# Layer 1 of the last two token groups: three units of four column tiles by seven products of halves

## The chip, the cores and the metric

The kernel runs on one core of a Trainium2 chip. The metric is the device time of one execution in microseconds (us); less is better.

## The reference

Attention with a relative-position bias for 8 batches, 8 heads, 576 positions and 64 numbers per head, followed by a feed-forward block on the 4608 rows of 512 numbers that it gives:

```python
scores = q @ k.T / 8 + bias_table[bucket(|i - j|)]
x = softmax(scores) @ v            # (8, 8, 576, 64) -> (4608, 512)
h = np.maximum(x @ w_in, 0.0)      # layer 1: 512 -> 2048
out = (h * h) @ w_out              # layer 2: 2048 -> 512
```

The change is in layer 1, `relu(x @ w_in)` and the squaring, for the last 1024 of the 4608 rows.

## The kernel before

The kernel writes down every operation with its engine, an estimated duration, what it depends on, the buffers it takes and a due time (`P.add`). A planner (`Plan.schedule`) then gives each engine a fixed order: the operation that can begin first goes first, and among those the one with the earliest due time. The engines execute that order; the planner's times themselves play no part on the chip, and semaphores hold an instruction back until its data is there. Each engine works its own queue strictly in order.

Attention goes by 32 pairs of heads (`pair(p)`, four to a batch): scores on TensorE (PE) into the PSUM tiles `sets_ps` (two tiles `st0`, `st1` of two banks each), exponentials on ScalarE (ACT) into one of three large buffers `pt`, the bias as a factor on VectorE (DVE), then `pv` matmuls and the division by the sum. The result `xs` is turned by a transposing DMA into `xt_sb` (512 numbers on 4 x 128 partitions, tokens along the row).

The two layers go by nine groups of 512 tokens (`layers(g)`, g from 0 to 8). Layer 1 of a group is 16 column tiles `nt` of 128 outputs. Each is a "quartet" of four matmuls (`f1`, line 1102: four slices `kk` of the 512 inputs, 512 tokens), into one of three banks `f` (`g_ps`). ACT takes the ReLU out of PSUM into `rt` (line 1123), and DVE squares it into `g` (line 1133), the group's activations.

Layer 2 (`second(g)`, line 1017) already goes by seven products of half matrices in place of eight (Winograd's form of Strassen's scheme): with the sums of activations `s` made on DVE (`sums_of_activations`, line 972) and sums of weights `wt` made once, products 1, 2, 6, 5, 7, 3, 4 go into PSUM, in two blocks of eight matmuls over 256 columns each, and DVE (line 1045) or ACT (line 1051) reads them into `y`, adding what was read before. Layer 2 of group g - 1 is planned among layer 1 of group g. In the last group it stands alone at the end.

The last `pv` matmuls end at 311.5 us of the profiled execution. After that only layer 2 of group 6 (its end), layer 1 of groups 7 and 8, and layer 2 of groups 7 and 8 are left. The three `pt` buffers and the two `st` tiles have no further use then.

Of the kernel before, what the change touches and what calls it, by code (L numbers as in the profile page):

```python
# [10 lines left out]
FP32 = mybir.dt.float32  # L11
FP16 = mybir.dt.float16
EXPF = mybir.ActivationFunctionType.Exp
RELUF = mybir.ActivationFunctionType.Relu
COPYF = mybir.ActivationFunctionType.Copy
MULT = mybir.AluOpType.mult

B, H, S, D = 8, 8, 576, 64
# [7 lines left out]
GT = 512  # L26
NG = B * S // GT
XB = 3
XR = XB * S
# [10 lines left out]
SIX = 2  # L40
V_EARLY, V_HW = 18900.0, 2
LATE2 = 7000
T_POOL, T_DUE = 0, 0
ORDER = "k0 i0 q1 q0 v i1 o0 k1 i2 o1 o2 i3 o3"
HALF = GT // 2
# [135 lines left out]
def mm(n):  # L181
    return n / 2.4 + 2.5


def act(n):
    return 174.0 + n / 1.2


def dve(n, rate=1.0, fix=160.0):
    return fix + n / (0.96 * rate)  # L190
# [3 lines left out]
def kernel(  # L194
# [10 lines left out]
    nc = tc.nc  # L205
    assert (_bucket(np.arange(128, S)) == NBK - 1).all()

    def io(ins):
        tc.keep_in_program_order(ins)
        return ins  # L210
# [16 lines left out]
    w_in_sb = sb("w_in_sb", [128, 4, 2048])  # L227
# [13 lines left out]
    pt_sb, pm_sb = sb("pt", [128, NPT, PW + 64]), sb("pm", [128, NPT, S + 64])  # L241
# [4 lines left out]
    xt_sb = sb("xt", [128, 4, XR + 64])  # L246
    wt_sb = sb("wt", [128, 3, 8, 256])
    ss = {i: sb(f"s{i}", [128, 8, 2, 128]) for i in (1, 2, 4)}
    gs = [sb(f"g{i}", [128, 16, GT]) for i in range(NGB)]
# [4 lines left out]
    rts = [sb(f"rt{i}", [128, GT]) for i in range(NRT)]  # L254
# [29 lines left out]
    def one_of(engs, fn, deps, bufs, due):  # L284
        op = P.add(engs, None, deps, bufs, due)
        op.fn = lambda: fn(op)
        return op
# [322 lines left out]

    xt_ready, x_last = {}, {}
    x_bufs = {}

    def copy_to(engs_n, out_f, in_f, deps, bufs, due, fp16=True, dve_only=False):

# [13 lines left out]
    def pair(p):  # L629
# [190 lines left out]
        for part, qt0, nq in ((0, 0, 3), (1, 3, 2)):  # L820
            bank = Buf(r_pv)

            def pv(qt0=qt0, nq=nq, bank=bank):
                ps = pv_ps[bank.slot][:, 0 : nq * 130].rearrange("p (t e d) -> p t e d", t=nq, e=2)
                pt, pm = pts[pb.slot], p4s[pb.slot]
                va, vm = vas[b_v[b].slot], v4s[b_v[b].slot]
                for i in range(nq):
                    c = (qt0 + i) * 128
                    io(
                        nc.tensor.matmul(  # L830
                            ps[:, i, :, :], pm[:, c : c + 128], vm[:, hp, :, 0:65], start=True, stop=False
                        )
                    )
                    for e in range(2):
                        for jt in range(4):
                            io(
                                nc.tensor.matmul(  # L837
                                    ps[:, i, e, :],
                                    pt[:, (2 * jt + e) * S + c : (2 * jt + e) * S + c + 128],
                                    va[:, jt, 2 * hp + e, 0:65],  # L840
                                    start=False,
                                    stop=(jt == 3 and e == 1),
                                )
                            )

            o = P.add(
                {"PE": nq * 300.0}, pv,
                bands + list(exps.values()) + l_v[b, hp] + first, [bank, pb, b_v[b]], T + 1, after, "f",
            )
            rb = Buf(r_r)  # L850

            def recip(nq=nq, bank=bank, rb=rb):
                ps = pv_ps[bank.slot][:, 0 : nq * 130].rearrange("p (t e d) -> p t e d", t=nq, e=2)
                io(nc.vector.reciprocal(out=rs[rb.slot][:, 0:nq], in_=ps[:, :, :, 64:65]))

            def norm(nq=nq, bank=bank, rb=rb, qt0=qt0):
                ps = pv_ps[bank.slot][:, 0 : nq * 130].rearrange("p (t e d) -> p t e d", t=nq, e=2)
                io(
                    nc.vector.tensor_tensor(  # L859
                        out=xs[xb.slot][:, qt0 : qt0 + nq, :].rearrange("p t (e d) -> p t e d", e=2),  # L860
                        in0=ps[:, :, :, 0:64],
                        in1=rs[rb.slot][:, 0:nq].to_broadcast([128, nq, 2, 64]),
                        op=MULT,
                    )
                )

            o = P.add({"DVE": 200.0}, recip, [o], [bank, rb], T - 2000)
            o = P.add({"DVE": dve(nq * 128)}, norm, [o], [bank, rb, xb], T - 2000)
            norms.append(o)
            if b >= DT_X:  # L870
                c = (b % XB) * S + 128 * qt0
                t = P.add(
                    {"SP": 1320.0},
                    lambda qt0=qt0, nq=nq, c=c: io(
                        nc.sync.dma_start_transpose(
                            out=xt_sb[:, hp, c : c + 128 * nq].rearrange("p (t d) -> p t d", d=128), in_=xs[xb.slot][:, qt0 : qt0 + nq, :].rearrange("p t d -> p (t d)")
                        )
                    ),
                    [o, x_last.get((hp, 1 - part))] + xt_free(b * S + 128 * (qt0 + nq)), [xb], T - 2000,
                )  # L880
                t = x_last[hp, part] = P.add({"DMA": 232.0 * nq}, None, [t], [xb], -1e9)
                end = b * S + min(128 * (qt0 + nq), S) - 1
                for g_ in range((b * S + 128 * qt0) // GT, end // GT + 1):
                    xt_ready.setdefault(g_, []).append(t)
# [48 lines left out]
    def sums_of_weights():  # L933
# [21 lines left out]
            done.append(o)  # L955
        return done

    def sums_of_activations(g):

        gb = g_bufs[g]  # L960
        sb_ = s_bufs[g] = {i: Buf(r_s[i]) for i in (1, 2, 4)}
        for c0 in (0, 4):
            o = None
            for to, uses in ((1, [1]), (2, [1, 2]), (4, [2, 4]), (3, [])):

                def add(to=to, c0=c0):
                    a11, a12, a21, a22 = (fourth(gb, eo, t, c0, 4) for t in range(2) for eo in range(2))
                    s = {i: ss[i][:, c0 : c0 + 4] for i in (1, 2, 4)}
                    out_, a, b_ = {
                        1: (s[1], a21, a22), 2: (s[2], a11, s[1]), 4: (s[4], a12, s[2]), 3: (a21, a21, a11)  # L970
                    }[to]
                    io(nc.vector.tensor_tensor(out=out_, in0=a, in1=b_, op=mybir.AluOpType.subtract))  # L972

                o = P.add(
                    {"DVE": dve(1024, 2.0)}, add, squares[g][2 * c0 : 2 * c0 + 8] + [o],
                    [gb] + [sb_[i] for i in uses], G0 + GP * g - 5e4,
                )
                s_done.setdefault((g, to), []).append(o)

    def second(g):  # L980
# [25 lines left out]
        for i in (int(x) for x in (P_LAST if g == NG - 1 else P_ORDER).split()):  # L1006
# [4 lines left out]
            for s_ in range(2):  # L1011
# [10 lines left out]
                        )  # L1022

                def atom(d, i=i, s_=s_, bf=bf, ns=ns, mul=mul, own=own):
                    deps = d + [x for n in ns for x in s_done[g, n]] + squares[g]
                    deps += read_of[before[i]] if i in before and not own else []
                    deps += l_wout if i in (1, 2) else t_done
                    return P.add(
                        {"PE": 8 * mm(HALF)}, mul, deps, [bf, gb] + [sb_[n] for n in ns if n != 3], 1e6, 0.0, "f",
                    )  # L1030
# [50 lines left out]
                atoms.append(fin)  # L1081
        return atoms

    def layers(g):

        due = G0 + GP * g
# [2 lines left out]
        if g < NG:  # L1089
            g_bufs[g] = Buf(r_gb)  # L1090
            gb1 = g_bufs[g]
            squares[g] = []
            for nt in range(16):
                bank = Buf(r_g)

                def f1(nt=nt, bank=bank):
                    c = (g * GT) % XR
                    n = min(GT, XR - c)
                    for a, z, c in ((0, n, c), (n, GT, 0)):
                        for kk in range(4 if z > a else 0):  # L1100
                            io(
                                nc.tensor.matmul(  # L1102
                                    g_ps[bank.slot][:, a:z], w_in_sb[:, kk, ts(nt, 128)],
                                    xt_sb[:, kk, c : c + z - a],
                                    start=(kk == 0), stop=(kk == 3),
                                )
                            )

                atoms1.append((nt, f1, bank))
        i2 = 0  # L1110
        last = None
        for i in range(16):
            if i < len(atoms1):
                nt, f1, bank = atoms1[i]
                o = P.add(
                    {"PE": 4 * mm(512)}, f1, xt_ready[g] + [l_win[nt // 4]], [bank, gb1], due + i * 2000, 0.0, "f"
                )
# [3 lines left out]
                def relu(o, bank=bank, rb=rb):  # L1121
# [4 lines left out]

                engs = {"ACT": act(512), "DVE": dve(512)} if g < RELU_DVE else {"ACT": act(512)}
                r = one_of(engs, relu, [o], [bank, rb], 0.0)
                squares[g].append(
                    P.add(  # L1130
                        {"DVE": dve(512, 2.0)},
                        lambda rb=rb, nt=nt, gb1=gb1: io(
# [64 lines left out]
```

## Time and profile before

| what | value |
|---|---|
| three runs | 372.94, 373.65, 372.58 us; median 372.94 |
| profiled execution | 372.94 us, of them a span of 371.1 us from the first to the last instruction |
| PE busy | 355.1 us (96%), 3930 matmuls |
| DVE busy | 265.8 us (72%) |
| ACT busy | 257.5 us (69%) |
| granted PE clock | 0.999 |
| last matmul | issued by about 368.0 us |

A row of the timeline gives start, duration, engine, line, operation, output and inputs with their shapes, and in brackets how long the engine was idle before it and which instruction ended that idle time. Matmuls are pipelined: the row of a merged run of matmuls also holds the time in which the last one drains, so the distance between starts is what a matmul costs PE. In the chain of work that ended last that part is left out. "Issue" as a releaser means that nothing in the profile held the engine back.

### The profile page before, as it was taken

The page shows a single profiled execution, that of the slowest core. Times are in us where ns is not written, and L with a number is a line of the kernel's source. Part 1 is how long each engine was busy: PE and PEld are TensorE (multiplying, and loading weights), DVE is VectorE, ACT ScalarE, POOL GpSimd, SP SyncE. Part 2 cuts the span into 40 slices and gives each one's busy share as a digit, 9 for nine tenths or more (in the row PEclk, how much of TensorE's full clock was granted, in tenths as well). Part 3 has the DMA queues.
Part 4 walks back from the last instruction along what each step waited for, and adds up shares of the span by engine and source line. Part 5 has one row for each costly group of instructions (what it writes and reads, how often), then busy time and mean ns, then how long its engine had stood idle before and what let it go on. Part 6 is the DMA issues. An engine that isn't in the chain of part 4 may idle for free.

```text
span 371.1 us, 9910 instructions
## 1 busy us (share of the span) xinstructions
PE 355.1 (96%) x3930; PEld 242.0 (65%) x3930; DVE 265.8 (72%) x594; ACT 257.5 (69%) x367; POOL 186.5 (50%) x343
## 2 busy tenths in 40 slices
PE   3978999899999999999999999999999999999996
PEld 2655555556587457877785468745877688546785
DVE  3997789957785598668965797569765985583573
ACT  4998989688575887679766887688659870564220
POOL 7897359194665686757846557667624100000000
PEclk9999999999999999999999999999999999999999
DMA  8999999595999999998999999999965224100022
GB/s 164 153 133 170 195 178 94 82 123 93 181 134 126 148 149 128 133 159 163 121 135 147 104 160 135 133 163 153 122 105 125 53 50 72 57 2 28 30 85 87
DMA packets 162292, 44.25 MB, mean 119 GB/s; under 512 B 145734, under 2 KB 162246, under 8 KB 162246
## 3 DMA queue, kind: packets, MB, share of 16 engines
q0 software_dynamic: 74208, 14.53, 50.7%
q1 hardware_dynamic: 87696, 28.80, 41.3%
q8 instruction: 31, 0.51, 0.6%
q10 hardware_dynamic: 342, 0.30, 0.3%
q14 instruction: 15, 0.12, 0.1%
HBM read 36.88 MB, written 9.44 MB: 125 GB/s over the span
## 4 chain that ended last, share of the span: by engine, by line
PE 86%; DVE 4%; DMA 4%; ACT 2%; POOL 2%; issue 1%; POOLq 0%; ACTq 0%
PE f L1102 34%; PE f L1017 29%; PE pv L837 9%; PE st L702 8%; PE pv L830 2%; DMA w_in_sb<-in_moe_w_in_dram 2%; PE st L751 2%; PE st L726 1%; DMA ks<-in_k_dram 1%; DVE pt L794 1%; ACT pt L713 1%; DVE x L859 1%; POOL ks L276 1%; DVE s L972 1%; POOL qs L276 1%
## 5 line engine op out<-in xcount | busy, mean ns | idle before, releaser
L713 ACT ACTIVATE pt<-st 128x1024 f16<-128x1024 f32 x128 | 127.4, 1025 | 30.4 <-PE st L702 30.4
L1102 PE MATMUL f<-xt,w_in_sb 128*128 128x512 f16 (+4 forms) x704 | 138.6, 341 | 0.2 <-ACT xt L619 0.2
L1123 ACT ACTIVATE rt<-f 128x512 f16<-128x512 f32 x144 | 85.2, 602 | 49.3 <-PE f L1102 44.0
L1102 PEld LDWEIGHTS <-w_in_sb 128*128 128x128 f16 x704 | 62.6, 98 | 57.3 <-issue 12.2
L1133 DVE TENSOR_TENSOR g<-rt 128x512 f16<-128x512 f16 x144 | 64.9, 455 | 36.6 <-ACT rt L1123 35.9
L794 DVE TENSOR_TENSOR pt<-pt,tb_sb 128x1536 f16<-128x1536 f16 (+2 forms) x96 | 60.1, 635 | 14.8 <-ACT pt L713 14.1
L1017 PEld LDWEIGHTS <-g 128*128 128x128 f16 x576 | 54.6, 98 | 14.4 <-issue 4.7
L276 POOL DMA_DIRECT2D qs<-in_q_dram x79 | 55.4, 714 | 4.0 <-DMA w_out_sb<-in_moe_w_out_dram 2.5
L276 POOL DMA_DIRECT2D ks<-in_k_dram x79 | 55.2, 702 | 1.4 <-issue 1.2
L837 PE MATMUL pv<-va,pt 128*128 128x65 f16 x1280 | 54.6, 193 | 0.0
L837 PEld LDWEIGHTS <-pt 128*128 128x128 f16 x1280 | 50.2, 97 | 2.7 <-issue 1.0
L1045 DVE SCALAR_TENSOR_TENSOR y<-f,y 128x512 f32<-128x512 f32 (+1 forms) x47 | 31.4, 667 | 22.9 <-PE f L1017 21.5
L1017 PEld LDWEIGHTS <-s 128*128 128x128 f16 x432 | 41.2, 98 | 9.8 <-issue 2.5
L702 PE MATMUL st<-qt,kt 64*128 64x512 f16 x256 | 40.5, 387 | 0.8 <-ACT pm L761 0.4
L684 POOL COPY qz<-qt 64x64 f16<-64x64 f16 x61 | 19.1, 313 | 39.8 <-DMA qt<-qs 31.4
L684 POOL COPY qz<-kt 64x64 f16<-64x64 f16 x58 | 18.7, 322 | 38.9 <-DMA kt<-ks 30.4
L1017 PE MATMUL f<-wt,g 128*128 128x256 f16 x288 | 36.2, 273 | 0.0
L1017 PE MATMUL f<-w_out_sb,s 128*128 128x256 f16 x288 | 36.1, 273 | 0.0
L830 PE MATMUL pv<-vm,pm 128*128 128x130 f16 x160 | 35.3, 221 | 0.7 <-DVE x L859 0.6
L1017 PE MATMUL f<-w_out_sb,g 128*128 128x256 f16 x272 | 34.5, 273 | 0.7 <-ACT y L1051 0.7
L859 DVE TENSOR_TENSOR x<-pv,r 128x384 f16<-128x384 f32 x64 | 31.4, 490 | 2.0
L972 DVE TENSOR_TENSOR s<-g,s 128x1024 f16<-128x1024 f16 x36 | 26.0, 723 | 0.4
(66 smaller groups left out, 284.9 us busy)
## 6 DMA issues: line engine op xcount, KB each, us to landing
out_dram<-y SPq DMA_DIRECT2D x34, 256.0 KB, 2.3
f<-in_v_dram SPq DMA_DIRECT2D x24, 256.0 KB, 4.4
qs<-in_q_dram POOLq DMA_DIRECT2D x48, 64.0 KB, 4.5
ks<-in_k_dram POOLq DMA_DIRECT2D x48, 64.0 KB, 3.6
w_in_sb<-in_moe_w_in_dram POOLq DMA_DIRECT2D x4, 512.0 KB, 7.6
w_out_sb<-in_moe_w_out_dram POOLq DMA_DIRECT2D x4, 512.0 KB, 10.2
qs<-in_q_dram POOLq DMA_DIRECT2D x7, 144.0 KB, 5.0
ks<-in_k_dram POOLq DMA_DIRECT2D x7, 144.0 KB, 6.2
```

The source lines that it names most:

```text
L276: lambda: io(eng.dma_start(out=out_(), in_=in_())),
L684: io(eng.tensor_copy(out=dst[qb.slot][rw, rw], in_=src[qb.slot][rw, 512:576]))
L702: nc.tensor.matmul(sets_ps[st.slot][:, e, :], kt[rw, ts(jt, 128)], qt[rw, 0:512], start=True, stop=True,)
L713: nc.scalar.activation(out=p5(pts[pb.slot])[:, jt, :, 0:512], in_=sets_ps[st.slot], func=EXPF, scale=SCALE)
L794: io(nc.vector.tensor_tensor(out=a, in0=a, in1=t, op=MULT))
L830: nc.tensor.matmul(ps[:, i, :, :], pm[:, c : c + 128], vm[:, hp, :, 0:65], start=True, stop=False)
L837: nc.tensor.matmul(ps[:, i, e, :], pt[:, (2 * jt + e) * S + c : (2 * jt + e) * S + c + 128], va[:, jt, 2 * hp + e, 0:65], start=False, sto ...
L859: nc.vector.tensor_tensor(out=xs[xb.slot][:, qt0 : qt0 + nq, :].rearrange("p t (e d) -> p t e d", e=2), in0=ps[:, :, :, 0:64], in1=rs[rb.s ...
L1017: nc.tensor.matmul(home[bf.slot][:, ts(s_, HALF)], left(c, s_), right(c), start=(c == 0 and (s_ == 0 or apart) and (own or i not in before ...
L1102: nc.tensor.matmul(g_ps[bank.slot][:, a:z], w_in_sb[:, kk, ts(nt, 128)], xt_sb[:, kk, c : c + z - a], start=(kk == 0), stop=(kk == 3),)
L1123: io(nc.scalar.activation(out=rts[rb.slot], in_=g_ps[bank.slot], func=RELUF))
L1133: nc.vector.tensor_tensor(out=gs[gb1.slot][:, nt, :], in0=rts[rb.slot], in1=rts[rb.slot], op=MULT)
```

## The change

A "unit" here is two neighbouring column tiles of the first 1024 columns of `w_in` and the two that lie 1024 columns further on, for all 512 tokens of a group: in the kernel before, 4 quartets (16 matmuls of 512 columns). The changed kernel computes two units of group 7 (tiles 0 to 3 and 8 to 11) and one unit of group 8 (tiles 0, 1, 8, 9) by seven products of halves: the 512 inputs are halved (k), the columns (i) and the tokens (j) as well. A product is four matmuls over 256 columns. The other 8 tiles of group 7 and 12 of group 8 stay quartets.

The sums that this needs (four of tokens `t` for each group, four of weights `s` for each pair of tiles, the latter shared by the two groups) are made by DVE into the room of the `pt` buffers, once the last `pv` matmuls are done. The products go into the four banks of `st0` and `st1`: products 1 (with 2 added on top) and 6 into the two banks of one tile, 5 (then 3) and 7 (then 4) into those of the other. They are read by ACT (product 1 by a copy, product 2 by a ReLU) or by DVE, which adds a partial sum `y` read before; those `y` too lie in the room of `pt`. Sums that are results then get a ReLU on ACT, in place in `rt`, and a square on DVE or ACT, whichever the planner finds free. The dependence on the squares is now kept by tile. Nothing is changed in attention, layer 2's arithmetic or any DMA.

```diff
+UNITS = {7: 2, 8: 1}
+USTEP = 700.0
...
+    pv_last = []
...
+            if p >= 4 * B - 3:
+                pv_last.append(o)
...
+    def made(g, a, z):
+        return [x for nt in range(a, z) for x in squares[g][nt]]
...
-                    {"DVE": dve(1024, 2.0)}, add, squares[g][2 * c0 : 2 * c0 + 8] + [o],
+                    {"DVE": dve(1024, 2.0)}, add, made(g, 2 * c0, 2 * c0 + 8) + [o],
...
-                    deps = d + [x for n in ns for x in s_done[g, n]] + squares[g]
+                    deps = d + [x for n in ns for x in s_done[g, n]] + made(g, 0, 16)
...
+    late, r_late = {}, Ring(4)
+    def late_room():
+        a, b_, c_ = (pt_sb[:, i, 0:4096] for i in range(3))
+        assert max(UNITS.values()) <= 2
+        for i in range(1, 5):
+            late["s", i] = a[:, ts(i - 1, 1024)].rearrange("p (k c) -> p k c", k=2)
+            late["y", i - 1] = b_.bitcast(FP32)[:, ts(i - 1, 512)]
+        for g in UNITS:
+            for i in range(1, 5):
+                o = ((g - min(UNITS)) * 4 + i - 1) * 512
+                late["t", g, i] = c_[:, o : o + 512].rearrange("p (k c) -> p k c", k=2)
+    def late_sums(n, dst, terms, deps, due):
+        o, made_ = None, []
+        for i, (a, b_, op) in terms:
+            o = P.add(
+                {"DVE": dve(n, 2.0)},
+                lambda i=i, a=a, b_=b_, op=op: io(nc.vector.tensor_tensor(out=dst(i), in0=a(), in1=b_(), op=op)),
+                deps + [o], (), due,
+            )
+            made_.append(o)
+        return made_
+    SUB = mybir.AluOpType.subtract
+    def by_sevens(g, units, due):
+        if not late:
+            late_room()
+        c = (g * GT) % XR
+        assert c + GT <= XR
+        wq = lambda i, k, u: w_in_sb[:, 2 * k : 2 * k + 2, 1024 * i + 256 * u : 1024 * i + 256 * u + 256]
+        xq = lambda k, j: xt_sb[:, 2 * k : 2 * k + 2, c + HALF * j : c + HALF * j + HALF]
+        t = lambda i: late["t", g, i]
+        t_ops = late_sums(
+            512, t,
+            [
+                (1, (lambda: xq(0, 1), lambda: xq(0, 0), SUB)),
+                (2, (lambda: xq(1, 1), lambda: t(1), SUB)),
+                (4, (lambda: xq(1, 0), lambda: t(2), SUB)),
+                (3, (lambda: xq(1, 1), lambda: xq(0, 1), SUB)),
+            ],
+            xt_ready[g] + pv_last, due - 1e5,
+        )
+        gb1 = g_bufs[g]
+        for u in range(units):
+            s_ = lambda i, u=u: late["s", i][:, :, ts(u, 256)]
+            if ("ops", u) not in late:
+                late["ops", u] = late_sums(
+                    512, s_,
+                    [
+                        (1, (lambda u=u: wq(1, 0, u), lambda u=u: wq(1, 1, u), mybir.AluOpType.add)),
+                        (2, (lambda s_=s_: s_(1), lambda u=u: wq(0, 0, u), SUB)),
+                        (4, (lambda u=u: wq(0, 1, u), lambda s_=s_: s_(2), SUB)),
+                        (3, (lambda u=u: wq(0, 0, u), lambda u=u: wq(1, 0, u), SUB)),
+                    ],
+                    l_win + pv_last, due - 1e5 + 10.0 * u,
+                )
+            sets = {"ab": Buf(r_set), "cd": Buf(r_set)}
+            y = {i: Buf(r_late) for i in "uv"}
+            prod = {
+                1: ("a", lambda u=u: wq(0, 0, u), lambda: xq(0, 0), True),
+                6: ("b", lambda s_=s_: s_(2), lambda: t(2), True),
+                2: ("a", lambda u=u: wq(0, 1, u), lambda: xq(1, 0), False),
+                5: ("c", lambda s_=s_: s_(1), lambda: t(1), True),
+                7: ("d", lambda s_=s_: s_(3), lambda: t(3), True),
+                3: ("c", lambda s_=s_: s_(4), lambda: xq(1, 1), False),
+                4: ("d", lambda u=u: wq(1, 1, u), lambda: t(4), False),
+            }
+            reads = {
+                1: ("u", None, None), 6: ("u", "u", None), 2: (None, None, (0, 0)), 5: ("v", "u", None),
+                7: (None, "v", (1, 1)), 3: (None, "u", (0, 1)), 4: (None, "u", (1, 0)),
+            }
+            after_read = {2: 1, 3: 5, 4: 7}
+            read_of = {}
+            for n, i in enumerate((1, 6, 2, 5, 7, 3, 4)):
+                bk, left, right, first_ = prod[i]
+                st = sets["ab" if bk in "ab" else "cd"]
+                ps = lambda st=st, bk=bk: sets_ps[st.slot][:, "abcd".index(bk) % 2, :]
+                def mul(left=left, right=right, first_=first_, ps=ps):
+                    for f in range(2):
+                        for kk in range(2):
+                            io(
+                                nc.tensor.matmul(
+                                    ps()[:, ts(f, HALF)], left()[:, kk, ts(f, 128)], right()[:, kk, :],
+                                    start=(first_ and f == 0 and kk == 0), stop=(kk == 1), skip_group_check=True,
+                                )
+                            )
+                o = f1_last[g] = P.add(
+                    {"PE": 4 * mm(HALF)}, mul,
+                    xt_ready[g] + t_ops + late["ops", u] + (read_of[after_read[i]] if i in after_read else []),
+                    [st, gb1], due + (7 * u + n) * USTEP, 0.0, "f",
+                )
+                to, plus, where = reads[i]
+                deps = [o]
+                if plus == "u":
+                    deps += read_of[1 if i == 6 else 6]
+                if plus == "v":
+                    deps += read_of[5]
+                bufs = [st] + [y[x] for x in {to, plus} - {None}]
+                rb = Buf(r_rt) if where else None
+                bufs += [rb] if rb else []
+                def ev(e, to=to, plus=plus, ps=ps, y=y, rb=rb):
+                    dst = rts[rb.slot] if rb else late["y", y[to].slot]
+                    if plus is not None:
+                        io(
+                            nc.vector.scalar_tensor_tensor(
+                                out=dst, in0=ps(), scalar=1.0, in1=late["y", y[plus].slot], op0=MULT, op1=mybir.AluOpType.add
+                            )
+                        )
+                    else:
+                        io(nc.scalar.activation(out=dst, in_=ps(), func=RELUF if rb else COPYF))
+                e = one_of({"DVE": dve(512)} if plus else {"ACT": act(512)}, ev, deps, bufs, 0.0)
+                read_of[i] = [e]
+                if not rb:
+                    continue
+                if plus is not None:
+                    e = P.add(
+                        {"ACT": act(512)},
+                        lambda rb=rb: io(nc.scalar.activation(out=rts[rb.slot], in_=rts[rb.slot], func=RELUF)),
+                        [e], [rb], 0.0,
+                    )
+                def square(o, rb=rb, where=where, u=u):
+                    src = rts[rb.slot].rearrange("p (f s) -> p f s", f=2)
+                    n0 = 8 * where[0] + 2 * u
+                    dst = gs[gb1.slot][:, n0 : n0 + 2, ts(where[1], HALF)]
+                    if o.eng == "ACT":
+                        io(nc.scalar.activation(out=dst, in_=src, func=SQUAREF))
+                    else:
+                        io(nc.vector.tensor_tensor(out=dst, in0=src, in1=src, op=MULT))
+                e = one_of({"DVE": dve(512, 2.0), "ACT": act(512)}, square, [e], [rb, gb1], due - 1e5)
+                for f in range(2):
+                    squares[g][8 * where[0] + 2 * u + f].append(e)
     def layers(g):
...
-            squares[g] = []
-            for nt in range(16):
+            squares[g] = {nt: [] for nt in range(16)}
+            units = UNITS.get(g, 0)
+            for nt in [nt for nt in range(16) if nt % 8 >= 2 * units]:
...
                 atoms1.append((nt, f1, bank))
+            if units:
+                by_sevens(g, units, due)
...
+        skip = 16 - len(atoms1) if g < NG else 0
         for i in range(16):
-            if i < len(atoms1):
-                nt, f1, bank = atoms1[i]
+            if i >= skip and g < NG:
+                nt, f1, bank = atoms1[i - skip]
...
-                squares[g].append(
+                squares[g][nt].append(
```

More of the change, by code (lines that the diff above doesn't have):

```diff
@@ L14 @@
 RELUF = mybir.ActivationFunctionType.Relu
+SQUAREF = mybir.ActivationFunctionType.Square
 COPYF = mybir.ActivationFunctionType.Copy
```

## The prediction

> **What bounds the kernel now.** I read the page's forty slices first, then the chain of work that ended last, then the windows of the last 58 us, then single rows of the timeline there. The built order of both programs is the same on SyncE and GpSimd throughout, and on TensorE, VectorE and ScalarE up to about 312 us, so only the tail can move.
>
> ```profile
> PE   3978999899999999999999999999999999999996
> DVE  3997789957785598668965797569765985583573
> ACT  4998989688575887679766887688659870564220
> ```
>
> ```profile
> 313.00:318.00 5.00, 5.00 (x37) 3.33 (x35) 1.66 (x4) 1.55 (x3) 0.00 (x0) 1.00 0.42 124
> 318.00:333.00 15.00, 15.00 (x74) 6.93 (x72) 10.70 (x24) 9.79 (x17) 0.00 (x0) 1.00 0.05 17
> 333.00:357.00 24.00, 24.00 (x175) 16.93 (x174) 12.96 (x26) 8.96 (x15) 0.00 (x0) 1.00 0.10 34
> ```
>
> The columns are the stretch, its length, then busy time of PE, weight loads, DVE, ACT, POOL, then the granted clock, the DMA share and GB/s. From 313 us PE is busy for the whole of each stretch at full clock, while DVE and ACT have room. The chain says the same: one unbroken run of matmuls.
>
> ```profile
> 318.48 14.68 PE f L1102 x68
> 333.15 0.87 PE f L1017 x8
> 359.24 8.75 PE f L1017 x80
> ```
>
> So here a matmul column taken out is time won, and a wait put in front of PE is time lost. In the before there is no such wait.
>
> **What it takes away.** A unit was 4 column tiles of layer 1, each a quartet of matmuls over 512 tokens. A quartet takes 0.866 us start to start (14.68 us over 17 quartets is 0.864), so 3.46 us a unit. It becomes 7 products of 4 matmuls over 256 columns. That shape stands in layer 2: 80 matmuls in 8.75 us, 0.109 us each, so a product is 0.436 us and a unit 28 x 0.109 = 3.05 us. Saved: 0.41 us a unit, 1.23 us for three units. The operands (w_in, xt, and sums in pt) are new in this shape; half of a 512 matmul (0.108) and the 0.109 row bound it closely. The built order has 36 more matmuls, which is 3 x (28 - 16): the change does what it says.
>
> A rule speaks against the exchange: the Trainium skill, "TensorE: Matmul & The Clock Gate", section "Back-to-back issue gap", puts sustained pairs of weight load and matmul at about 131 ns for 512 columns and 81 ns for 128, so small moving operands pay for their weight loads. By it, as an estimate with 98 ns put in for 256, a unit would cost 0.6 us more instead of less. The rows above show 216 and 109 ns, in proportion, and they decide.
>
> **What it adds beside PE.** DVE: 16 sums in half precision (4 for each group's tokens, 4 for each of the two weight slices) at 0.41 us each (a 512-element sum of two SBUF operands has such rows), 15 additions out of PSUM at 0.69 us, less 6 squares of 0.42 us that go to ACT: 14 us. ACT: 3 copies and 6 squares more at 0.60 us: 5 us. The squares and the ReLU from SBUF have no row; 0.60 us (PSUM source) is the nearest, and taking 0.42 to 0.70 moves the result by less than 0.1 us, as most lie beside matmuls. The 4 sums for group 7 and the first weight slice fit DVE's gaps between 312 and 317 us (it is busy 1.66 us of 313 to 318), ahead of the first product that reads them at 317.9. GpSimd and SyncE get nothing, and no DMA is moved. So the volume is covered; what counts is waits.
>
> **The waits.** These rows price one hop each: four matmuls, then ACT reading their bank, then DVE reading what ACT wrote.
>
> ```profile
> 313.98 1.03 PE L1102 MATMUL f<-xt,w_in_sb 128*128 128x512 f16 x4
> 315.04 0.60 ACT L1123 ACTIVATE rt<-f 128x512 f16<-128x512 f32 x1 [9.34 <-PE f L1102]
> 315.67 0.42 DVE L1133 TENSOR_TENSOR g<-rt 128x512 f16<-128x512 f16 x1 [0.80 <-ACT rt L1123]
> 140.61 0.42 DVE L859 TENSOR_TENSOR x<-pv,r 128x256 f16<-128x256 f32 x1
> 141.09 0.22 PE L830 MATMUL pv<-vm,pm 128*128 128x130 f16 x1 [0.21 <-DVE x L859]
> L1045 DVE SCALAR_TENSOR_TENSOR y<-f,y 128x512 f32<-128x512 f32 x11 | 7.6, 689 | 5.4 <-PE f L1017 4.3 <-DMA xt<-x 1.1
> ```
>
> From the end of issue of the last matmul (313.98 + 0.87 = 314.85) to ACT's start is 0.20; ACT to DVE 0.03; DVE to PE 0.06.
>
> By the built order the products of the first and third unit run 1, 6, 5, 7, 2, then other work, 3, 4; of the second 1, 6, other work, 2, 5, 7, a quartet, 3, a quartet, 4. Products 1 and 6 lie in the two banks of one PSUM tile, 5 and 7 in those of the other. In the built program, waits go by tile and not by bank: ACT's copy of product 1 waits for product 6 too, and product 2 (which accumulates onto 1) waits for the addition that reads product 6. So product 2 can start only after product 6, copy, addition:
> 0.20 + 0.60 + 0.03 + 0.69 + 0.05 = 1.57 us after 6 has been issued.
> PE has products 5 and 7 meanwhile: 0.87 us. Stall 0.70 us. Queued behind product 2 on PE stands everything else, the plain quartets too, as the queue is in order. In the same way product 3 waits for the additions that read 5 and then 7 (0.20 + 0.69 + 0.03 + 0.69 + 0.05 = 1.66 us after 7), and product 4 for the one that reads 3 (0.94 us after 3).
>
> I walked the three queues of the built order from 312 us with these durations. The same walk of the before gives no stall and an end of PE at 368.04 us; the trace has 359.24 + 8.75 = 367.99. For the changed order it gives:
> - group 7, first unit: product 2 stalls 0.69; products 3 and 4 have two plain quartets (1.73) ahead of them and stall nothing;
> - group 7, second unit: between 6 and 2 stand a quartet and a block of layer 2 (1.74), but ACT and DVE are still finishing the first unit: 0.22; product 3 has only one quartet (0.87) against 1.66: 0.79; product 4, a quartet against 0.94: 0.07;
> - group 8, its unit: product 2 again 0.69; product 3 0.13; product 4 0.06.
>
> Sum 2.65 us. Net: 2.65 - 1.23 = +1.42 us. After the last product (about 341 us) the walk has no more waits: all of layer 1 is now ahead of layer 2's products 6 to 4 of group 7, which run 8.7 us and cover the squares and sums of group 8. The 1.42 us therefore reaches the end, and the output DMAs follow as before. The profiled execution took 372.94 us (span 371.1 and 1.84 around it), which is also the median of the three runs. So 372.94 + 1.42 = 374.4 us.
>
> Bounds: if nothing queued on ACT and DVE and each hop cost nothing, only the three large stalls would be left, about 0.6 + 0.65 + 0.6, and the net would be +0.6 us (373.6). If each of the seven waits cost 0.1 us and each of its additions 0.05 us more, the stalls would be 3.7 us, the net +2.5 (375.4).
>
> **The rivals.** A difference of under 0.3% (1.12 us) is about what a measurement of this kernel can't tell from no change.
>
> *No wait decides* (other side, faster). If product 2 waited for the copy of product 1 alone, the chain would be 0.20 + 0.60 + 0.05 = 0.85 us counted from product 1, and products 6, 5 and 7 (1.31) would cover it; with the like for 3 and 4 only the 1.23 us would be left: 371.7 us. It decides when the stalls of a unit are below 0.41 us. For it: DVE's free 4.3 of 15 us and ACT's 5.2. Against it: the waits of the built order are by tile, and idle time elsewhere does not shorten a chain of dependent steps. Chance 0.07.
>
> *Stalls and saving nearly cancel.* Stalls between 0.1 and 2.35 us, for instance if the 0.79 or one of the 0.69 is absent because a plain quartet that follows has cover: about 373.6 us. Chance 0.26.
>
> *More than the walk.* Square might need another function table than the one loaded at the start, which took 1.28 us here: 375.7 us with one more load. The built order has no further load. The Trainium skill, "ScalarE: Activation LUTs", section "Table sets: the hidden batching unit", gives about 2.7 us for a switch; the one load in this trace took 1.28 us, and that is what I use. Or ACT, with 9.79 us busy of 15 before, falls behind on group 7 and holds layer 2's first product: that product stands at about 334.2, the last square of group 7 at about 332.7, so ACT and DVE may be 1.5 us late before this costs. Chance 0.05, 375 to 376 us.
>
> *The forecast*, 1.1 to 2.5 us slower: chance 0.62.
>
> **How the numbers follow.** Slower by over 0.3%: forecast and the last rival, 0.67. Within 0.3%: 0.26. Faster: 0.07. The range: bounds 373.6 to 375.4, widened at the low end into the cancelling case, and by the scatter of the medians (runs from 372.58 to 373.65): 373.1 to 375.5. Outside it I leave the faster rival, the low end of the cancelling case and the far tail of the last, under 0.2.
>
> **What would show it.** Right: PE idle 2.2 to 3.2 us in all before the new matmuls, released by DVE; three waits of 0.6 to 0.9 us (two before product 2 at about 319.9 and 338.2, one before product 3 at about 328.7); new products 0.109 us a matmul; the run from the last layer-2 matmul to the end unchanged; clock still 1.00. Wrong: no idle PE between 318 and 342 us (then faster), new matmuls above 0.115 us (saving gone without any wait), a second table load, or a wait in front of group 7's layer 2.

## The result, and the profile after

The changed kernel takes 375.07 us (median of 6 runs, 374.18 to 375.31), the kernel before 372.81 us beside it (6 runs): ratio 1.0054, 95% interval 1.0040 to 1.0069, so 1.5 to 2.6 us slower. Forecast was 374.4 us, slower, in a range of 373.1 to 375.5.

The slices and two of the stretches of the changed kernel, in the same columns as before:

```profile
PE   3978999899999999999999999999999999999996
DVE  3897789967775598668865786579755877788773
ACT  4998989688575887679767887688568860777300
318.00:333.00 15.00, 13.73 (x94) 9.00 (x93) 11.72 (x24) 11.19 (x21) 0.00 (x0) 1.00 0.06 19
333.00:357.00 24.00, 23.41 (x174) 16.79 (x173) 20.15 (x41) 11.78 (x21) 0.00 (x0) 1.00 0.06 21
```

The slices still show 9 for PE up to the last one: a tenth of a slice is 0.9 us, and the new waits are shorter. Only the stretches show that PE now pauses: 13.73 of 15 us and 23.41 of 24, where both had been full. The clock stays at 1.00. DVE's work has grown from 12.96 to 20.15 of the 24 us of the second stretch and still leaves it idle time.

PE's own timeline from the first new product to the last (start, duration, line, output and inputs, runs merged; line 1183 is a new product, 1258 a plain quartet, 1027 layer 2):

```profile
318.03 0.60 PE L1183 MATMUL st<-xt,w_in_sb 128*128 128x256 f16 x4
318.46 1.47 PE L1183 MATMUL st<-pt 128*128 128x256 f16 x12
320.52 0.60 PE L1183 MATMUL st<-xt,w_in_sb 128*128 128x256 f16 x4 [0.59 <-DVE pt L1208]
...
325.30 1.04 PE L1027 MATMUL f<-wt,g 128*128 128x256 f16 x8
326.38 0.60 PE L1183 MATMUL st<-xt,w_in_sb 128*128 128x256 f16 x4
326.81 1.04 PE L1183 MATMUL st<-pt 128*128 128x256 f16 x8
327.69 1.03 PE L1258 MATMUL f<-xt,w_in_sb 128*128 128x512 f16 x4
329.35 0.60 PE L1183 MATMUL st<-xt,pt 128*128 128x256 f16 x4 [0.64 <-DVE rt L1208]
329.79 1.03 PE L1258 MATMUL f<-xt,w_in_sb 128*128 128x512 f16 x4
330.80 0.60 PE L1183 MATMUL st<-pt,w_in_sb 128*128 128x256 f16 x4
...
336.87 1.47 PE L1183 MATMUL st<-pt 128*128 128x256 f16 x12
338.88 0.60 PE L1183 MATMUL st<-xt,w_in_sb 128*128 128x256 f16 x4 [0.54 <-DVE pt L1208]
```

Products 6, 5 and 7 start at 318.46 and need 12 x 0.109 = 1.31 us; product 2 could begin at 319.77 and begins at 320.52. That is a wait of 0.75 us. The bracket says 0.59, because the profile lets a matmul's row last 0.16 us longer than its place in the queue. Read in this way, from start to start, the waits before the new products are 0.75, 0.21, 0.80, 0.15, 0.70, 0.21 and 0.07 us, 2.9 in all. The brackets alone would give 1.8.

The start of that first wait, as it looks on the two engines that end it:

```profile
319.15 0.60 ACT L1213 ACTIVATE pt<-st 128x512 f32<-128x512 f32 x1 [0.33 <-PE st L1183]
319.78 1.49 DVE L1208 SCALAR_TENSOR_TENSOR pt<-st,pt 128x512 f32<-128x512 f32 x2 [0.50 <-ACT pt L1213]
```

Product 1 was issued by 318.46, but ACT's copy of it begins at 319.15, after product 6 (issued by 318.90, drained 0.16 us later); DVE's first addition begins 0.03 us after the copy, and PE goes on 0.05 us after that addition (319.78 + 0.69 = 320.47).

From the first matmul of group 7's layer 1 to the start of the last block of layer 2 the kernel before took 366.06 - 313.98 = 52.08 us, the changed one 368.34 - 314.56 = 53.78: +1.70 us. On PE the built order differs in this stretch and nowhere else. The remaining 0.6 us of the two profiled spans lies ahead of it, where both kernels do the same; the experiments show how much that part varies by itself.

### The profile page after: what moved, and what is told of

It reads as the page before. It is cut to its first block, busy times and chain, and to the rows that moved or that the text cites. A ratio compares the mean times of both kernels' runs of the same rounds, so it can differ in the third digit from the quotient of the medians.

```text
span 373.4 us, 10016 instructions
## 1 busy us (share of the span) xinstructions
PE 355.4 (95%) x3966; PEld 245.9 (66%) x3966; DVE 278.0 (74%) x619; ACT 261.6 (70%) x376; POOL 185.3 (50%) x343
## 4 chain that ended last, share of the span: by engine, by line
PE 85%; DVE 9%; DMA 3%; ACT 2%; issue 1%; ACTq 0%; DVEq 0%
PE f L1258 31%; PE f L1027 27%; PE pv L841 9%; PE st L706 8%; PE pv L834 2%; PE st L1183 2%; DVE pt L798 2%; PE st L755 2%; DMA xt<-x 1%; PE st L730 1%; DVE x L865 1%; DMA g<-in_q_dram 1%; DVE pt L1208 1%; PE f L661 1%; DVE rt L1208 1%; ACT pm L765 1%
## 5 line engine op out<-in xcount | busy, mean ns | idle before, releaser
L717 ACT ACTIVATE pt<-st 128x1024 f16<-128x1024 f32 x128 | 127.4, 1024 | 30.9 <-PE st L706 30.8
L1258 PE MATMUL f<-xt,w_in_sb 128*128 128x512 f16 (+4 forms) x656 | 127.5, 338 | 0.7 <-DMA xt<-x 0.4
L1282 ACT ACTIVATE rt<-f 128x512 f16<-128x512 f32 x132 | 77.8, 601 | 34.7 <-PE f L1258 30.8
L1258 PEld LDWEIGHTS <-w_in_sb 128*128 128x128 f16 x656 | 57.9, 98 | 52.7 <-issue 12.2
L1292 DVE TENSOR_TENSOR g<-rt 128x512 f16<-128x512 f16 x132 | 58.2, 449 | 21.7 <-ACT rt L1282 20.5
```

Of the source, the lines that this page charges most:

```text
L717: nc.scalar.activation(out=p5(pts[pb.slot])[:, jt, :, 0:512], in_=sets_ps[st.slot], func=EXPF, scale=SCALE)
L1258: nc.tensor.matmul(g_ps[bank.slot][:, a:z], w_in_sb[:, kk, ts(nt, 128)], xt_sb[:, kk, c : c + z - a], start=(kk == 0), stop=(kk == 3),)
L1282: io(nc.scalar.activation(out=rts[rb.slot], in_=g_ps[bank.slot], func=RELUF))
L1292: nc.vector.tensor_tensor(out=gs[gb1.slot][:, nt, :], in0=rts[rb.slot], in1=rts[rb.slot], op=MULT)
```

## The experiments

Every kernel is read in two ways: by its ratio to the kernel before, and by the stretch just named, which leaves out what happens before 314 us. The theory is "waits by tile": PE waits because a product that is added onto another waits for every reader of the PSUM tile, and its chain (matmul, copy, addition) is longer than what PE has in front. The rival is "volume": DVE and ACT have too much to do, in whatever order and tile.

**1. Product 1 in a tile of its own.**

```diff
+            apart = {"a": (pv_ps, Buf(r_pv))}
...
-                st = sets["ab" if bk in "ab" else "cd"]
-                ps = lambda st=st, bk=bk: sets_ps[st.slot][:, "abcd".index(bk) % 2, :]
+                room, st = apart.get(bk, (None, sets["ab" if bk in "ab" else "cd"]))
+                ps = lambda st=st, bk=bk, room=room: (
+                    room[st.slot] if room else sets_ps[st.slot][:, "abcd".index(bk) % 2, :]
+                )
```

> Product 1 (and 2 on top of it) goes into the PSUM tile that attention's pv matmuls left free, so it no longer shares a tile with product 6; 5, 7, 3 and 4 share theirs as in the change. Theory 'waits by tile': product 2 now waits for ACT's copy of product 1 alone (0.85 us after 1 is issued, 1.31 us of products 6, 5, 7 in front), so its three stalls (0.75, 0.21, 0.70 us in the changed kernel's trace) go; about 1.2 to 1.4 us of stalls before products 3 and 4 stay. Net against the kernel before: +0.2 us, 373.0. Rival 'volume' (DVE and ACT have too much work, whichever tile is used): the work is the same, so the time stays at the changed kernel's, +1.7 to +2.2 us, 374.5 to 375.0.

Measured: 373.06 us, ratio 1.0008 (0.9991 to 1.0026), the stretch 52.44 us, +0.36. In the stretch PE's instructions stand in exactly the order of the changed kernel; only the tile of products 1 and 2 differs. DVE's and ACT's instructions keep their order too. PE's timeline of the first unit and of the next wait:

```profile
317.73 1.47 PE L1186 MATMUL st<-pt 128*128 128x256 f16 x12
319.04 0.60 PE L1186 MATMUL pv<-xt,w_in_sb 128*128 128x256 f16 x4
...
326.00 1.03 PE L1261 MATMUL f<-xt,w_in_sb 128*128 128x512 f16 x4
327.67 0.60 PE L1186 MATMUL st<-xt,pt 128*128 128x256 f16 x4 [0.64 <-DVE rt L1211]
```

Product 2 now follows at 317.73 + 1.31 = 319.04, without a gap. Product 3, whose tile is shared as before, still waits: 327.67 - 326.87 = 0.80 us. The waits left are 0.80, 0.15, 0.53 and 0.08 us. With the work on DVE and ACT unchanged in amount and order, this is against "volume".

**2. Four tiles for the four running products.** The same edit, and

```diff
-            apart = {"a": (pv_ps, Buf(r_pv))}
+            apart = {"a": (pv_ps, Buf(r_pv)), "d": (g_ps, Buf(r_g))}
```

> As the run before, and products 7 and 4 also leave the shared tile for one of the three f banks: products 1, 6, 5, 7 lie in four tiles. Theory 'waits by tile': no stall of PE before any of the new products; the saving of 3 x 0.41 us alone is left: -1.2 us, 371.6. It could lose 0.1 to 0.4 us of that if two f banks are too few for the plain quartets. Rival 'volume': +1.7 to +2.2 us, as the work on DVE and ACT is the same.

Measured: 371.96 us, ratio 0.9964 (0.9949 to 0.9980); the stretch 50.89 us, -1.19, where the saving of the columns alone would be -1.23. Two stretches of its profile:

```profile
318.00:333.00 15.00, 15.00 (x103) 9.88 (x101) 13.43 (x29) 12.02 (x23) 0.00 (x0) 1.00 0.08 26
333.00:357.00 24.00, 24.00 (x190) 18.40 (x189) 21.40 (x41) 11.01 (x20) 0.00 (x0) 1.00 0.10 34
```

PE is full again, although DVE is busier in both stretches than in the changed kernel (13.43 against 11.72 us, 21.40 against 20.15), and ACT in the first (12.02 against 11.19): with PE not held up, more of their work falls into the same time. But the planner has also changed PE's order here: between products 7 and 3 stand 2.2 us of other work in the second and in the third unit, where run 1 has 0.9 and 1.3 and the prediction counted 1.66 for the chain. Run 1 sets the tile apart from the order; for the waits that were left, this run does not.

**3. The old tiles, the planner told of the true waits.**

```diff
-            after_read = {2: 1, 3: 5, 4: 7}
+            after_read = {2: 6, 3: 7, 4: 3}
```

> Tiles, instructions and engines as in the change, but the planner is told the waits that tiles really make (product 2 after the addition that reads 6, 3 after the one that reads 7, 4 after the one that reads 3), and so puts quartets and layer 2 blocks in front of the waiting products. Theory 'waits by tile' with uncovered PE: the chains take as long as before but PE works meanwhile: stalls under 0.3 us before the new products; in exchange about 0.6 us at layer 2's first product of group 8 or thereabouts: net -0.6 us, 372.2. Rival 'volume': the same work in another order, +1.5 to +2.2 us.

Measured: 372.47 us, ratio 0.9982 (0.9966 to 0.9998); the stretch 51.61 us, -0.47. PE's timeline, with the first unit and the longest wait that is left:

```profile
319.02 1.47 PE L1183 MATMUL st<-pt 128*128 128x256 f16 x12
320.33 1.03 PE L1258 MATMUL f<-xt,w_in_sb 128*128 128x512 f16 x4
321.19 0.60 PE L1183 MATMUL st<-xt,w_in_sb 128*128 128x256 f16 x4
...
347.78 0.60 PE L1027 MATMUL f<-wt,s 128*128 128x256 f16 x4
348.82 1.48 PE L1027 MATMUL f<-wt,s 128*128 128x256 f16 x12 [0.44 <-DVE s L982]
```

A quartet stands where the gap was, and product 2 follows it at once. The chains are as long as in the changed kernel; what differs is that PE has work in front. Before the new products one wait of 0.11 us is left. The price is what was forecast: the plain work used as cover is missing later, and layer 2 of group 7 waits for DVE's sums (product 6, 348.82 - 348.22 = 0.60 us from start to start). I had placed that wait at layer 2 of group 8, wrongly.

**4. Four units with four tiles.** The second run with `UNITS = {7: 2, 8: 2}`.

> Four tiles as in the second run, and a second unit of group 8 by seven products, four units in all. Theory 'waits by tile': a unit without stalls is worth 0.41 us: -1.6 us, 371.2. Rival 'volume': one more unit on DVE (5 additions, about 3 us more work) is worse than three units, by 0.5 us or more, so +2.2 us or more; a weaker form: with DVE fuller, the fourth unit brings nothing against the second run.

Measured: 371.27 us, ratio 0.9951 (0.9932 to 0.9971), the stretch 50.50 us, -1.58: 0.39 us less than three units. This is the fastest version here by its median and by the stretch; the intervals of its ratio and of run 2's overlap.

**5. and 6. One group at a time, tiles as in the change.** `UNITS = {7: 2}` and `UNITS = {8: 1}`.

> The change with the two units of group 7 alone (group 8 all by plain quartets), tiles as in the change. Theory 'waits by tile': saving 0.82 us, stalls as in the changed kernel's group 7 (0.75 + 0.21 + 0.80 + 0.15 = 1.9 us): net +1.0 to +1.1 us against the kernel before. Rival 'volume': the loss goes with the number of units, two thirds of the change's 1.7 us: +1.1 us, so this run alone does not tell them apart; its idle rows of PE do.

> The change with the one unit of group 8 alone. The planner then puts other work behind the first two products, so that product 2 is covered and product 3 is the one that stalls, by 0.64 us with the durations of the trace. Theory 'waits by tile': 0.64 - 0.41 = +0.2 us, no change that can be measured. Rival 'volume', one third of 1.7 us: +0.6 us.

Measured for group 7 alone: the stretch 53.19 us, +1.11, with the first and third of the changed kernel's long waits in it (0.59 and 0.65 by the brackets) at the same places. Its time is 375.57 us, ratio 1.0061 (1.0041 to 1.0080), which is more than +1.11 us accounts for. Part of that is the granted clock: three of its six executions were granted 0.995 and took 375.87 to 376.20 us, the three at 1.00 took 374.33 to 375.26. The median of those three, 374.69, is 1.4 us above the 373.28 of the kernel before at 0.999 or more in the same round. In its profile the end is also later: 5.8 us from the start of the last block to the end of the span, 5.0 in the kernel before, with the last output DMAs landing in a median of 2.5 us after issue in place of 1.7. Why they were slower there stays open; the order at the end is the same.

For group 8 alone: 373.58 us, ratio 1.0016 (1.0003 to 1.0030), the stretch 52.41 us, +0.33, and a single wait, before product 3, as forecast: 0.73 us from start to start (0.57 by the bracket), where 0.64 was forecast. 0.73 - 0.41 is the +0.33 but for 0.01; "volume" had +0.6. The two stretches add up to 1.44 us against 1.70 for both, the difference being the other order of group 8.

**7. Six units with four tiles.** Three units in each group, the partial sums in a ring of three.

> Four tiles as in the second run, and three units in each of the two groups, six in all (a ring of three in place of four for the partial sums read). Theory 'waits by tile' alone, without regard to the volume: 6 x 0.41 = -2.5 us. With the volume: DVE now has 5 additions, 8 sums and 4 ReLU-fed squares per unit, which in the order of the planner keep PE waiting by about 7 us in many waits of 0.2 to 0.9 us: net +4.5 us, 377. So it shows where DVE's and ACT's work does become the bound.

Measured: 378.11 us, ratio 1.0141 (1.0111 to 1.0171), the stretch 56.94 us, +4.86, with 16 waits of PE, 7.2 us in all from start to start. (The sums are 20 for all six units, 8 of tokens and 12 of weights, not 8 a unit as the expectation says.) One of its stretches, and the longest of PE's waits in the tail (total us, times, longest):

```profile
333.00:357.00 24.00, 19.94 (x163) 15.59 (x163) 23.21 (x43) 21.25 (x39) 0.00 (x0) 1.00 0.04 12
PE f L1027 <- ACT g L1239: 1.4, 1, 1.4
PE f L1191 <- DVE pt L1121: 0.8, 1, 0.8
PE f L1027 <- DVE g L1241: 0.6, 1, 0.6
```

Here the rival fits: DVE is busy for 23.21 of 24 us and ACT for 21.25, PE for 19.94, and PE's waits are ended by DVE and ACT. The bound has moved from PE to these two engines. In the second and fourth run DVE had about 21.4 of 24 us and PE lost nothing; between four and six units the exchange turns over. The ring of three is a second difference of this run, and its share was not measured apart.

**8. The changed kernel again.**

> The changed kernel itself once more, to see what of its time is the stretch before the change: the same seven waits as in its first trace (2.9 us in all, within 0.1 us), the same 53.8 us from the first matmul of group 7's layer 1 to the last product; the start of that stretch (314.56 us in the first trace, 313.98 in the kernel before) is expected anywhere from 313.6 to 315.1, as in the four runs so far. Time +1.5 to +2.3 us.

Measured: 375.31 us, ratio 1.0061 (1.0040 to 1.0083); the stretch 53.77 us against 53.78 in the first trace, and the same three bracketed waits (0.58, 0.64, 0.54). The stretch began at 314.01 us, against 314.56 in the first trace of this same kernel. So the 0.6 us ahead of the stretch was no effect of the change.

The stretch in all kernels (from the start of group 7's layer 1 to the start of the last block; "forecast" is what each expectation gave for it or for the net):

| kernel | begins at | stretch | against before | forecast |
|---|---|---|---|---|
| before | 313.98 | 52.08 | | |
| changed | 314.56 | 53.78 | +1.70 | +1.42 |
| changed again | 314.01 | 53.77 | +1.69 | +1.7 |
| 1: product 1 apart | 313.83 | 52.44 | +0.36 | +0.2 |
| 2: four tiles | 314.83 | 50.89 | -1.19 | -1.2 |
| 3: planner told | 315.12 | 51.61 | -0.47 | -0.6 |
| 4: four tiles, four units | 313.61 | 50.50 | -1.58 | -1.6 |
| 5: group 7 alone | 313.83 | 53.19 | +1.11 | +1.0 to 1.1 |
| 6: group 8 alone | 315.58 | 52.41 | +0.33 | +0.2 |
| 7: four tiles, six units | 316.87 | 56.94 | +4.86 | +4.5 |

## Why the prediction was right, and where it was off

**The saving.** Forecast 1.23 us, shown: with the waits gone (run 2) the stretch is 1.19 us shorter, and a fourth unit is worth 0.39. Twelve new matmuls take 1.31 us (run 1, 317.73 to 319.04), 0.109 each, and so do those with operands from `w_in` and `xt` (four in 0.43 us, 318.03 to 318.46 in the changed kernel). Matmuls of 512 columns stand 216 ns apart (16 from 331.24 to 334.69). The sustained figures of the Trainium skill, "TensorE: Matmul & The Clock Gate", section "Back-to-back issue gap", 131 ns for 512 columns and 81 ns for 128, are not what these rows show. Halving the moving operand halved the time, and the measurement decides.

**The waits.** Forecast seven waits of 0.69, 0.22, 0.79, 0.07, 0.69, 0.13 and 0.06 us, 2.65 in all; measured 0.75, 0.21, 0.80, 0.15, 0.70, 0.21 and 0.07, 2.9 in all, at the forecast products. That they come from the shared tiles is shown by run 1, which changes the tile and not PE's order, for the three before product 2; for the four before products 3 and 4 it is read off their rows, since run 2, where they are gone, changes the order as well. That they cost only what is uncovered is shown by run 3.

**The size.** The stretch is 0.28 us longer than forecast: the saving is 0.04 us smaller and the waits are 0.24 longer. Three hops (the time from one step of a chain to the next), each taken too short, make up most of the 0.24. The rows that price them, from the changed kernel, are these beside those above:

```profile
327.88 0.69 DVE L1208 SCALAR_TENSOR_TENSOR pt<-st,pt 128x512 f32<-128x512 f32 x1 [0.63 <-PE st L1183]
328.61 0.69 DVE L1208 SCALAR_TENSOR_TENSOR rt<-st,pt 128x512 f16<-128x512 f32 x1
330.06 0.69 DVE L1208 SCALAR_TENSOR_TENSOR rt<-st,pt 128x512 f16<-128x512 f32 x1 [0.42 <-ACT rt L1222]
337.51 0.60 ACT L1213 ACTIVATE pt<-st 128x512 f32<-128x512 f32 x1 [0.28 <-PE st L1183]
338.14 1.49 DVE L1208 SCALAR_TENSOR_TENSOR pt<-st,pt 128x512 f32<-128x512 f32 x2 [1.14 <-ACT pt L1213]
```

- Before product 2 of the first unit (0.06 us more): ACT's copy begins 0.25 us after product 6 has been issued (318.90 to 319.15), where I took 0.20. In the third unit it is 0.20 (337.31 to 337.51), and that wait came within 0.01.
- Before product 3 of the third unit (0.08 more): the addition that reads product 5 begins 0.10 us after the one that reads 6 has ended (the two take 1.49 us, 0.69 each), where I took 0.03 from one addition to the next. From the one that reads 5 to the one that reads 7 it is 0.03 to 0.04 (327.88 + 0.69 to 328.61).
- Before product 4 of the second unit (0.08 more): the addition that reads product 3 begins 0.27 us after that product's issue (329.79 to 330.06), where I took 0.20, and the bracket says that ACT's ReLU in `rt` released it.

Why the same hop differs from unit to unit stays open. ReLU and Square from SBUF took 0.61 to 0.63 us, not 0.60, mostly off the path.

**The rest of the time.** The measured ratio stands for 2.0 us (1.5 to 2.6), the stretch for 1.70, so nothing more need be explained. The prediction counted on a scatter of the medians but had no cause for it; the runs show where it lies: mostly ahead of the stretch, once (run 5) behind it.

**The rivals.** "No wait decides" was wrong for this kernel, and its price was right: run 2 is that case, with other work in front as well, and its stretch is 1.19 us shorter. "Stalls and saving nearly cancel" is run 1. Of "more than the walk", no second table load appears (one, of 1.28 us, at 2.7 us of the span), and layer 2 of group 7 was not held up (its first block starts at 334.69, right after 3.62 us of quartets from 331.24).

**The marker.** I had written that PE idle would sum to 2.2 to 3.2 us. From start to start it does (2.9); the brackets of the profile add up to 1.8 us, since it ends a matmul's row after its drain. A reader with the waits table alone would have called the forecast too high.

## What to carry to other kernels

A cheaper algorithm on the bound engine brings its saving only if what it adds, the intermediate reads, has other work in front of it on that engine: count, for each dependent matmul, the chain (drain, copy, addition, semaphore) and the work that is queued between, in the built order. Products that run at the same time belong in PSUM tiles of their own, since the built program's waits go by tile (run 1); where they can't, tell the planner the waits that tiles make. Then add units until the helping engines are full, here somewhere between four and six (six were run with a shorter ring as well).

## What the runs showed that was not expected

The part ahead of the change varies by itself: the same instructions in the same order reach the start of the stretch between 313.61 and 316.87 us in ten profiled executions. Much of that is there early: one `pv` matmul of the first third begins between 113.58 and 115.30 us in the ten, and the three latest, 114.90 to 115.30, are those of runs 3, 6 and 7. In these three PE's granted clock was 0.51 to 0.57 from 26 to 29.4 us, and 1.00 in the other seven. The rows of run 3 and of the changed kernel (the clock is the third number from the end):

```profile
26.00:29.40 3.40, 3.40 (x55) 2.36 (x51) 3.08 (x8) 2.43 (x3) 3.08 (x6) 0.51 1.45 95
26.00:29.40 3.40, 3.03 (x75) 2.40 (x74) 3.19 (x9) 2.89 (x4) 2.85 (x5) 1.00 1.19 74
```

From a matmul at about 22 us to one at about 31 us these three took 10.0 us or a little more, the others 8.1 to 8.9. They also reach the stretch latest, at 315.12, 315.58 and 316.87 us, the others from 313.61 to 314.83. So the clock is one cause of the scatter, and it differs between executions of one kernel: in the last round the kernel before was granted 0.994 or 0.995 in 4 of its 19, with a median of 374.03 us against 373.28. Single waits come in between, such as 0.4 us for a late transposing DMA at 119.7 us in the first trace of the changed kernel, 0.8 us for GpSimd's copies into `qz` in run 2 and 1.3 us in run 7. For a change of half a per cent, the stretch between two matmuls that both kernels have was the better measure: in the one changed kernel profiled twice it repeated within 0.01 us.
